# A planner that keeps GpSimd and VectorE apart in SBUF, block products that wait for their own sums, and new due times: a three-stage fp32 kernel on one Trainium2 core

## The chip, the core and the metric

The kernel runs on one core of a Trainium2 chip. The metric is the device time of one launch in microseconds (us). The time before is the median of 3 runs, 641.36 us (641.22, 641.36 and 764.43). One further execution was profiled; it took 639.59 us, and its span from the first to the last instruction is 637.8 us.

Engines are named as in the profile: PE is TensorE's matmuls, PEld its weight loads, DVE is VectorE, ACT is ScalarE, POOL is GpSimd, SP is the queue that issues DMAs.

## The reference

Three stages follow each other. Attention over 2 batches of 8 heads with 768 positions of 64 (a local band of 96 keys and 8 global keys, with a slope per head) gives x with 1536 rows of 512. Network 1 and network 2 each multiply by 512 x 2048, apply a function, and multiply by 2048 x 512.

```python
scores = scale * np.matmul(q, k.transpose(0, 1, 3, 2))
bias = -slopes[:, None, None] * dist[None, :, :]
scores = np.where(keep, scores + bias[None], -1000000000.0)
a = np.exp(scores - np.max(scores, axis=-1, keepdims=True))
x = np.matmul(a / (np.sum(a, axis=-1, keepdims=True) + 1e-09), v)   # heads joined: 1536 x 512
h = x @ moe_w_in
g = np.where(h >= 1, h, np.where(h <= -1, 0.0, (h + 1) ** 2 / 4))
x = g @ moe_w_out
h = x @ moe2_w_in
out = np.maximum(0.01 * h, h) @ moe2_w_out
```

The weights arrive as 64-bit numbers, q, k and v as 32-bit ones.

## The kernel before

**Numbers in two halves.** A 32-bit matmul operand is held as a rounded half `[:, 0]` and a rest `[:, 1]`; every product takes three matmuls (half by half, half by rest, rest by half). So each operand needs a copy (`copy`, L206 on ACT, L208 on DVE) and a subtraction (`sub`, L212 on DVE, L214 on POOL).

**Weights.** `job` turns one 128 x 512 piece of 64-bit weights into its halves. One DMA fills `raw`; `s0` (L407 or L409), `s01` (L413), `s1` (L417), `s11` (L421) build the number's upper part in `wd`, `s2` (L425) its lower part in `wr`, `s3` (L428, an integer addition that only POOL may do) adds them; `s4` and `s5` are the copy and the subtraction into the ring `w`. There are 64 such jobs. For network 2, `sums` (L468) also makes two combinations of each pair of pieces.

**Attention.** 24 calls of `quad` handle four heads of 128 positions each: transposes of k and q (L525), evictions into `ks` and `qt`, scores (L557), the table and the maximum (L566), exp (L575), row sums (L580, L581), normalization (L588 on DVE, L590 on POOL), transposes (L599), the product with v (L612), the eviction into `x`. Until the first four quads are through, the planner fills idle places of PE with dummy matmuls (L354).

**Network 1.** `step` does one 128-wide piece f of the hidden layer for one unit of rows: the hidden product (L693), `a1` (L700), the square (L708 or L710), `a2` (L715, which frees the PSUM bank), the two halves into `g`, then the output products (L755) into four banks; `finish` adds them to `part` (L792) and, at the last group, makes the halves of x anew. There are 6 units of 256 rows for the first 2 pieces f, then 3 units of 512 rows (twice, 7 pieces each). Unit 2 of 512 rows comes last.

**Passage and network 2.** For units 0 and 1 the hidden layer of network 2 is made from seven block products instead of eight. `x_sums` (L844) makes four sums t1, t2, t3, t4 of blocks of x and splits each into halves, t1 in the place of part of `x[1]`, t2, t3, t4 in the tiles `xt`. `two(j, True)` then runs, for each of 8 rounds j, seven products of six matmuls (L885) on four PSUM banks, with two VectorE additions from bank to bank between them (`cc`, L930, and `ce`, L933):

```python
p1 = add({PE: c6}, prod(Ba, wa, 0, x0, 0, True, False), d, w1 + xs, takes=[Ba, Bb, Bc, Be] + Hs)
p5 = add({PE: c6}, prod(Be, wc, 1, x1, 0, True, True), d + n7, [p1] + wx_op[j])
```

They go on in the order p2, p6 (t2), `cc`, p7 (t3), `ce`, p3, p4 (t4). `two(j, False)` does unit 2 with plain products (L952). Then come the activation (L896, L901) and the output products (L967); `finish` adds into `part` and, in the last round, writes out (L810, DMA).

**What sets the order.** Nothing above is issued as it stands. Each piece of work is an `Op` with a cost per engine that may do it, a due time (a table `DUE`, added to the due time of its step or round), the work that must precede it and the buffers that it takes and gives back. `Schedule.run` plays the program through with these costs: whenever an engine is idle, it gets the ready `Op` with the earliest due time whose buffers are free. The order so found is the order of each engine's queue on the chip; there only semaphores on data and buffers hold an instruction back, and the planned times play no part.

## Time and profile before

| | |
|---|---|
| median of 3 runs | 641.36 us |
| the profiled execution | 639.59 us, of which the span 637.8 us |
| busy PE / PEld | 615.7 us (97%) / 511.6 us (80%) |
| busy DVE / ACT / POOL | 500.7 us (79%) / 345.4 us (54%) / 291.0 us (46%) |
| mean granted TensorE clock | 0.984 of full speed |

Each share is a mean over the three stages, which differ. A dummy matmul counts as busy PE, and a matmul at the lower granted clock counts as busy for its longer time; so a view by stretch, with the granted clock beside the busy times, tells more than the page's first part. The mean of a group of instructions holds for the stretch that the view was asked for.

### The profile page before, as it was taken

The page shows a single profiled execution, that of the slowest core. Times are in us where ns is not written, and L with a number is a line of the kernel's source. Part 1 is how long each engine was busy: PE and PEld are TensorE (multiplying, and loading weights), DVE is VectorE, ACT ScalarE, POOL GpSimd, SP SyncE. Part 2 cuts the span into 40 slices and gives each one's busy share as a digit, 9 for nine tenths or more (in the row PEclk, how much of TensorE's full clock was granted, in tenths as well). Part 3 has the DMA queues.
Part 4 walks back from the last instruction along what each step waited for, and adds up shares of the span by engine and source line. Part 5 has one row for each costly group of instructions (what it writes and reads, how often), then busy time and mean ns, then how long its engine had stood idle before and what let it go on. Part 6 is the DMA issues. An engine that isn't in the chain of part 4 may idle for free.

```text
span 637.8 us, 9609 instructions
## 1 busy us (share of the span) xinstructions
PE 615.7 (97%) x3395; PEld 511.6 (80%) x3395; DVE 500.7 (79%) x985; ACT 345.4 (54%) x744; POOL 291.0 (46%) x314
## 2 busy tenths in 40 slices
PE   7999999999999999999999798999999999999995
PEld 5878887898688888888888686888888888888884
DVE  4899999979995649972559989668888888887653
ACT  3898898966464546553446445553536363534120
POOL 4477776447663234730116657306353536362000
PEclk7999999999999999999999988999999999999998
DMA  5974554113341203320012022102221212200014
GB/s 99 221 170 126 122 153 116 35 34 133 99 133 33 67 34 99 133 66 1 0 34 66 1 99 68 66 2 66 67 66 67 66 67 67 66 1 1 1 51 153
DMA packets 62346, 46.99 MB, mean 74 GB/s; under 512 B 40144, under 2 KB 56784, under 8 KB 62288
## 3 DMA queue, kind: packets, MB, share of 16 engines
q1 hardware_dynamic: 62288, 46.28, 25.0%
q8 instruction: 29, 0.48, 0.3%
q14 instruction: 29, 0.24, 0.1%
HBM read 43.12 MB, written 3.15 MB: 73 GB/s over the span
## 4 chain that ended last, share of the span: by engine, by line


## 5 line engine op out<-in xcount | busy, mean ns | idle before, releaser
L755 PE MATMUL bank<-g,w 128*128 128x512 f32 (+1 forms) x648 | 144.4, 369 | 0.0
L693 PE MATMUL bank<-x,w 128*128 128x512 f32 (+1 forms) x648 | 141.7, 368 | 2.2 <-POOL w L214 1.8
L693 PEld LDWEIGHTS bank<-x,w 128*128 128x128 f32 x648 | 111.8, 188 | 24.1 <-POOL w L214 2.9
L755 PEld LDWEIGHTS bank<-g,w 128*128 128x128 f32 x648 | 113.4, 189 | 21.3 <-issue 0.5
L428 POOL TENSOR_TENSOR wd<-wd,wr 128x512 int32<-128x512 int32 x64 | 88.9, 1395 | 77.2 <-DVE wd L421 72.5
L967 PE MATMUL bank<-w,g 128*128 128x512 f32 x312 | 81.8, 389 | 0.0
L792 DVE TENSOR_TENSOR part<-bank,part 128x512 f32<-128x512 f32 x96 | 65.1, 682 | 14.0 <-PE bank L755 8.9
L967 PE MATMUL bank<-w,w 128*128 128x512 f32 x264 | 70.6, 389 | 0.0
L700 ACT ACTIVATE t<-bank,half 128x512 f32<-128x512 f32 (+1 forms) x54 | 34.5, 639 | 63.5 <-PE bank L693 48.2
L214 POOL TENSOR_TENSOR g<-t,g 128x512 fp32r<-128x512 f32 (+1 forms) x32 | 37.9, 1185 | 67.9 <-ACT g L206 47.8
L967 PEld LDWEIGHTS bank<-w,g 128*128 128x128 f32 x312 | 58.6, 188 | 12.1
L206 ACT CAST w<-wd 128x512 fp32r<-128x512 f32 x50 | 31.0, 620 | 53.9 <-POOL wd L428 30.6
L206 ACT CAST g<-t 128x512 fp32r<-128x512 f32 (+1 forms) x73 | 43.0, 590 | 29.0 <-DVE t L901 13.4
L967 PEld LDWEIGHTS bank<-w,w 128*128 128x128 f32 x264 | 49.6, 188 | 10.3
L214 POOL TENSOR_TENSOR w<-wd,w 128x512 fp32r<-128x512 f32 x34 | 46.1, 1356 | 22.9 <-DVE w L208 12.9
L896 ACT ACTIVATE t<-bank 128x512 f32<-128x512 f32 x48 | 28.6, 597 | 51.4 <-DVE bank L933 25.9
L715 DVE SCALAR_TENSOR_TENSOR t<-bank,t 128x512 f32<-128x512 f32 (+1 forms) x54 | 33.7, 624 | 27.9 <-ACT t L708 25.9
L885 PE MATMUL bank<-x,w 128*128 128x512 f32 x192 | 52.1, 410 | 3.2 <-DVE t L715 3.2
L421 DVE SCALAR_TENSOR_TENSOR wd<-raw,wd 128x512 int32<-128x512 int32 x64 | 53.3, 845 | 0.5
L212 DVE TENSOR_TENSOR g<-t,g 128x512 fp32r<-128x512 f32 x48 | 42.8, 892 | 10.1 <-ACT g L206 9.3
L212 DVE TENSOR_TENSOR w<-wd,w 128x512 fp32r<-128x512 f32 x46 | 44.6, 978 | 6.5 <-ACT w L206 4.8
L425 ACT ACTIVATE wr<-raw 128x512 int32<-128x512 uint32 x64 | 43.1, 674 | 10.5 <-POOL wd L428 10.5
(113 smaller groups left out, 1012.8 us busy)
## 6 DMA issues: line engine op xcount, KB each, us to landing
raw<-in_moe_w_in_dram SPq DMA_DIRECT2D x32, 512.0 KB, 3.8
raw<-in_moe_w_out_dram SPq DMA_DIRECT2D x32, 512.0 KB, 3.5
kd<-in_k_dram SPq DMA_DIRECT2D x24, 128.0 KB, 3.2
qd<-in_q_dram SPq DMA_DIRECT2D x24, 128.0 KB, 3.2
vd<-in_v_dram SPq DMA_DIRECT2D x12, 256.0 KB, 3.8
out_dram<-part SPq DMA_DIRECT2D x11, 256.0 KB, 2.0
out_dram<-part SPq DMA_DIRECT2D x2, 128.0 KB, 3.1
vg<-in_v_dram SPq DMA_DIRECT2D x2, 64.0 KB, 3.6
```

The source lines that it names most:

```text
L206: A.copy(out=out_, in_=in_)
L212: V.tensor_tensor(out=out_, in0=a, in1=b, op=ALU.subtract)
L214: GP.tensor_tensor(out=out_, in0=a, in1=b, op=ALU.subtract)
L421: V.scalar_tensor_tensor(out=Dd.tile, in0=hl()[0], scalar=-0x40000000, in1=Dd.tile, op0=ALU.bitwise_and, op1=ALU.bitwise_or)
L425: A.activation(out=Rr.tile, in_=hl()[1], func=AF.Copy, scale=2.0 ** -29)
L428: GP.tensor_tensor(out=Dd.tile, in0=Dd.tile, in1=Rr.tile, op=ALU.add)
L693: T.matmul(out=Hb.tile[:, 0:n], lhsT=wi.tile[:, a, kk * P:(kk + 1) * P], rhs=x[r][:, b, kk, c0:c0 + n], start=(kk == 0 and a + b == 0), st ...
L700: A.activation(out=t, in_=h, func=AF.Relu, bias=half, scale=0.5)
L755: T.matmul(out=o[:, z * n:(z + 1) * n], lhsT=wo.tile[:, a, cc * P:(cc + 1) * P], rhs=Gt.tile[:, b, 0:n], start=st, stop=sp_)
L792: V.tensor_tensor(out=part[r][sl], in0=ac(), in1=part[r][sl], op=ALU.add)
L885: T.matmul(out=bank.tile, lhsT=w.tile[:, a, (2 * z + kk) * P:(2 * z + kk + 1) * P], rhs=xx()[:, b, kx + kk, :], start=st and kk == 0 and a ...
L967: T.matmul(out=Bo.tile, lhsT=Gt[z, r].tile[:, b, cb * P:(cb + 1) * P], rhs=wo[z].tile[:, a, :], start=(z == 0 and a + b == 0), stop=(z == ...
```

## The change

- `Schedule.run` gets a rule for SBUF: an `Op` of DVE that is not marked `ps` (has no operand in PSUM) starts only while POOL is idle in the plan, and an `Op` of POOL only when no such `Op` of DVE runs. 15 calls of `add` are marked.
- The planned costs of DVE and POOL are smaller (a 512-wide DVE operation from two SBUF tensors 0.60 us, was 0.64; a copy 0.33, was 0.43; POOL's 1.26, was 1.33).
- `s3` may go to DVE too.
- `x_sums` keeps a name for each sum, and each block product waits for its own: p1 for the first two blocks of unit 0 and for the first output products of unit 2's last group, p5 for t1, p2 for two blocks of unit 0, p6 for t2, p7 for t3, p3 for two blocks of unit 1, p4 for t4.
- Network 2's due times start earlier by `TWO`, and the whole table of due times is new.

```diff
@@ Schedule.run
+                        if e == DVE and not o.ps and busy[POOL] > now or e == POOL and held > now:
+                            kept.append(x)
...
+                            continue
...
+                    if e == DVE and not o.ps:
+                        held = end
@@ emit
     def dve(n, fast=False):
-        return 67 + (0.7 if fast else 1.12) * n
+        return 67 + (0.523 if fast else 1.044) * n
     def pool_tt(n):
-        return 200 + 2.2 * n
+        return 187 + 2.1 * n
...
+    z -= TWO
     for j in range(NJ):
@@ job
         def s3(e):
-            GP.tensor_tensor(out=Dd.tile, in0=Dd.tile, in1=Rr.tile, op=ALU.add)
+            (V if e == DVE else GP).tensor_tensor(out=Dd.tile, in0=Dd.tile, in1=Rr.tile, op=ALU.add)
...
-        e0 = add({POOL: pool_tt(DM)}, s3, due + DUE["s3"], [c1, r], gives=[Rr])
+        e0 = add(both(DM), s3, due + DUE["s3"], [c1, r], gives=[Rr])
@@ two
-            xs = [o for rr in (0, 256, 512, 768) for o in x2_op.get(rr, [])] + x2_op["sums"]
...
-            p1 = add({PE: c6}, prod(Ba, wa, 0, x0, 0, True, False), d, w1 + xs, takes=[Ba, Bb, Bc, Be] + Hs)
-            p5 = add({PE: c6}, prod(Be, wc, 1, x1, 0, True, True), d + n7, [p1] + wx_op[j])
+            p1 = add({PE: c6}, prod(Ba, wa, 0, x0, 0, True, False), d, w1 + [s_of[0, 0], s_of[0, 1]] + acc_op[0, last_g[0], LARGE[-1]],
+                     takes=[Ba, Bb, Bc, Be] + Hs)
+            p5 = add({PE: c6}, prod(Be, wc, 1, x1, 0, True, True), d + n7, [p1] + wx_op[j] + x2_op["t1"])
...
-            p7 = add({PE: c6}, prod(Bb, wc, 0, lambda: xt[1], 0, False, False), d + 4 * n7, [p6, cc])
+            p7 = add({PE: c6}, prod(Bb, wc, 0, lambda: xt[1], 0, False, False), d + 4 * n7, [cc] + x2_op["t3"])
...
-            p4 = add({PE: c6}, prod(Bb, wb, 1, lambda: xt[2], 0, False, True), d + 6 * n7, [p3, ce])
+            p4 = add({PE: c6}, prod(Bb, wb, 1, lambda: xt[2], 0, False, True), d + 6 * n7, [ce] + x2_op["t4"])
@@
-JTWO = 11218.0
-START = 9438.0
+JTWO = 9533.0
+TWO = 6956.0
+START = 4271.0
...
-DUE = {'b0': -23756.0, 'b1': 8444.0, 'b2': -94.0, 'b3': 5431.0, ...
+DUE = {'b0': -10861.0, 'b1': 24038.0, 'b2': 5854.0, 'b3': 8875.0, ...
```

By the number of instructions, POOL has 38 of the 64 integer additions `s3`, where it had all (DVE has the other 26), 26 of the 64 `s01`, where it had 38, and 58 of the 96 normalizations, where it had 66. In all it has 223 instructions instead of 315, DVE 1061 instead of 987, ACT 668 instead of 650. PE does the same matmuls, with 95 dummies instead of 83.

Three places show how instructions move. The first is PE's queue at the passage, from the hidden product whose bank p5 will use (unit 2, `x2`) to the second or third block product. Before:

```order
L693 MATMUL bank6_76<-x2_67,w0_7_2065 128x512 x12
L755 MATMUL bank7_77<-g1_95,w1_2_92 128x512 x3
L755 MATMUL bank4_74<-g3_97,w1_3_93 128x512 x3
L755 MATMUL bank1_71<-g1_95,w1_2_92 128x512 x3
L755 MATMUL bank2_72<-g3_97,w1_3_93 128x512 x3
L755 MATMUL bank4_74<-g2_96,w1_4_2066 128x512 x3
L755 MATMUL bank7_77<-g3_97,w1_3_93 128x512 x3
L885 MATMUL bank3_73<-x0_65,w0_1_87 128x512 x6
L755 MATMUL bank1_71<-g3_97,w1_3_93 128x512 x3
L755 MATMUL bank2_72<-g2_96,w1_4_2066 128x512 x3
L885 MATMUL bank6_76<-x1_66,w0_2_88 128x512 x6
```

And now (L707, L769 and L901 are the old L693, L755 and L885):

```order
L707 MATMUL bank5_75<-x2_67,w0_7_2094 128x512 x12
L769 MATMUL bank4_74<-g0_94,w1_3_93 128x512 x3
L769 MATMUL bank7_77<-g1_95,w1_4_2095 128x512 x3
L769 MATMUL bank6_76<-g1_95,w1_4_2095 128x512 x3
L769 MATMUL bank7_77<-g3_97,w1_5_2096 128x512 x3
L769 MATMUL bank0_70<-g1_95,w1_4_2095 128x512 x3
L901 MATMUL bank2_72<-x0_65,w0_0_86 128x512 x6
L769 MATMUL bank4_74<-g1_95,w1_4_2095 128x512 x3
L901 MATMUL bank5_75<-x1_66,w0_2_88 128x512 x6
L901 MATMUL bank2_72<-x0_65,w0_0_86 128x512 x6
```

Between that hidden product and p5, which takes its bank, stand 30 matmuls before and 24 now.

The second place is the same queue a little later, from p7 (`xt` 1) to p4 (`xt` 2) of the first round. Before:

```order
L885 MATMUL bank5_75<-xt1_2059,w0_2_88 128x512 x6
L755 MATMUL bank1_71<-g3_97,w1_7_2069 128x512 x3
L885 MATMUL bank0_70<-x1_66,w0_3_89 128x512 x6
L885 MATMUL bank5_75<-xt2_2060,w0_0_86 128x512 x6
```

Now:

```order
L901 MATMUL bank3_73<-xt1_2088,w0_2_88 128x512 x6
L769 MATMUL bank6_76<-g2_96,w1_6_2097 128x512 x3
L769 MATMUL bank0_70<-g3_97,w1_5_2096 128x512 x3
L901 MATMUL bank1_71<-x1_66,w0_3_89 128x512 x6
L769 MATMUL bank0_70<-g2_96,w1_6_2097 128x512 x3
L769 MATMUL bank4_74<-g3_97,w1_5_2096 128x512 x3
L769 MATMUL bank7_77<-g0_94,w1_7_2098 128x512 x3
L769 MATMUL bank4_74<-g2_96,w1_6_2097 128x512 x3
L769 MATMUL bank6_76<-g0_94,w1_7_2098 128x512 x3
L901 MATMUL bank3_73<-xt2_2089,w0_1_87 128x512 x6
```

Between p7 and p4 stand 9 matmuls before and 27 now.

The third place is PE's queue in a later round of network 2, again from p7 to p4. Before:

```order
L885 MATMUL bank1_71<-xt1_2059,w0_6_2064 128x512 x6
L967 MATMUL bank6_76<-w1_0_90,w1_4_2066 128x512 x3
L967 MATMUL bank6_76<-w1_1_91,g0_94 128x512 x3
L885 MATMUL bank3_73<-x1_66,w0_7_2065 128x512 x6
L967 MATMUL bank7_77<-w1_0_90,w1_4_2066 128x512 x3
L967 MATMUL bank7_77<-w1_1_91,g0_94 128x512 x3
L885 MATMUL bank1_71<-xt2_2060,w0_5_2063 128x512 x6
```

Now, from p6 (`xt` 0) on:

```order
L901 MATMUL bank2_72<-xt0_2087,w0_7_2094 128x512 x6
L983 MATMUL bank7_77<-w1_2_92,w1_3_93 128x512 x3
L983 MATMUL bank7_77<-w1_7_2098,w1_5_2096 128x512 x3
L901 MATMUL bank2_72<-xt1_2088,w0_6_2093 128x512 x6
L901 MATMUL bank1_71<-x1_66,w0_7_2094 128x512 x6
L901 MATMUL bank2_72<-xt2_2089,w0_5_2092 128x512 x6
```

Where 18 matmuls stood between p7 and p4, now 6 stand, in each of the seven rounds after the first. Between p6 and p7 stood 18 matmuls (30 in the first round); now there stand 6 in the first round and in three later ones, 12 in three and 24 in one.

## Rows read from the trace of the kernel before

**Rows 1.** The page, busy time of each engine, its share of the span, instructions.

```profile
PE 615.7 (97%) x3395; PEld 511.6 (80%) x3395; DVE 500.7 (79%) x985; ACT 345.4 (54%) x744; POOL 291.0 (46%) x314
```

**Rows 2.** Stretches of the span: length, busy time (instructions) per engine, granted clock.

```profile
core 0: us, PE busy (x) PEld busy (x) DVE busy (x) ACT busy (x) POOL busy (x), PEclk, DMA share, GB/s
9.30:43.20 33.90, 33.29 (x331) 27.32 (x331) 30.93 (x134) 28.69 (x104) 19.31 (x38) 0.90 0.84 191
43.20:139.00 95.80, 92.40 (x908) 80.74 (x907) 90.63 (x304) 84.38 (x256) 62.14 (x91) 1.00 0.40 104
139.00:355.00 216.00, 214.27 (x964) 177.07 (x963) 159.96 (x219) 112.24 (x185) 93.06 (x74) 1.00 0.21 66
...
365.00:371.00 6.00, 6.00 (x14) 4.73 (x15) 4.55 (x6) 1.31 (x3) 3.67 (x3) 0.50 0.29 87
...
384.00:392.00 8.00, 5.16 (x16) 3.77 (x15) 8.00 (x11) 4.31 (x8) 5.84 (x6) 0.79 0.21 67
392.00:631.20 239.20, 239.20 (x1056) 197.82 (x1054) 183.66 (x279) 102.38 (x173) 91.32 (x81) 1.00 0.16 54
```

**Rows 3.** What PE waited for: total us, times, longest.

```profile
PE bank L885 <- DVE t L715: 3.2, 1, 3.2
PE bank L885 <- DVE bank L933: 2.8, 1, 2.8
```

**Rows 4.** DVE's timeline before the first stall's end.

```profile
359.13 2.98 DVE L212 TENSOR_TENSOR xt<-part,xt 128x512 fp32r<-128x512 f32 x3
362.03 0.68 DVE L212 TENSOR_TENSOR g<-t,g 128x512 fp32r<-128x512 f32 x1
...
364.19 0.69 DVE L715 SCALAR_TENSOR_TENSOR t<-bank,t 128x512 f32<-128x512 f32 x1 [0.21 <-ACT t L708]
```

**Rows 5.** ACT's timeline at the same place.

```profile
362.81 0.69 ACT L700 ACTIVATE t<-bank,half 128x512 f32<-128x512 f32 x1 [6.12 <-DVE g L212]
```

**Rows 6.** DVE's timeline before the second stall's end.

```profile
384.72 1.52 DVE L409 TENSOR_SCALAR wd<-raw 128x512 int32<-128x512 int32 x1
386.16 0.41 DVE L417 TENSOR_SCALAR wd<-wd 128x512 int32<-128x512 int32 x1
386.50 0.69 DVE L933 TENSOR_TENSOR bank<-bank,s 128x512 f32<-128x512 f32 x1
```

**Rows 7.** Operations on the tiles x, w, wd, part: duration ns min/median/max.

```profile
L212 DVE TENSOR_TENSOR w<-wd,w x46: 677/693/1783, 139.6 to 586.3; 128x512 fp32r<-128x512 f32 x46
L421 DVE SCALAR_TENSOR_TENSOR wd<-raw,wd x64: 661/686/1787, 35.2 to 573.7; 128x512 int32<-128x512 int32 x64
L428 POOL TENSOR_TENSOR wd<-wd,wr x64: 1270/1295/1747, 39.5 to 574.6; 128x512 int32<-128x512 int32 x64
L792 DVE TENSOR_TENSOR part<-bank,part x96: 673/681/692, 192.6 to 614.9; 128x512 f32<-128x512 f32 x96
```

**Rows 8.** A later round: DVE's `ce` and PE's p7 and the blocks behind it.

```profile
412.09 1.52 PE L885 MATMUL bank<-xt,w 128*128 128x512 f32 x6
413.45 1.52 PE L967 MATMUL bank<-w,w 128*128 128x512 f32 x6
...
413.65 0.70 DVE L933 TENSOR_TENSOR bank<-bank,s 128x512 f32<-128x512 f32 x1 [4.74 <-PE bank L885]
```

**Rows 9.** Groups of DVE instructions in the attention stage, 9.3 to 139 us: busy us, mean ns.

```profile
L588 DVE TENSOR_SCALAR sm<-sm,st 128x256 f32<-128x256 f32 x24 | 10.7, 484 | 0.0
L580 DVE TENSOR_SCALAR st<-st 128x4 f32<-128x4 f32 x24 | 8.1, 338 | 0.0
L208 DVE COPY part<-bank 128x512 f32<-128x512 f32 x3 | 2.0, 679 | 0.0
L208 DVE CAST ks<-bank 128x256 fp32r<-128x256 f32 x4 | 1.6, 412 | 0.0
```

**Rows 10.** DVE's row sums (L580), same stretch: duration ns min/median/max.

```profile
L580 DVE TENSOR_SCALAR st<-st x24: 150/164/1270, 19.4 to 129.9; 128x4 f32<-128x4 f32 x24
```

**Rows 11.** DVE's timeline, the shortest pair of normalizations.

```profile
44.12 0.63 DVE L588 TENSOR_SCALAR sm<-sm,st 128x256 f32<-128x256 f32 x2
```

More of the change, by code (lines that the diff above doesn't have):

```diff
@@ L52 @@
 class Op:
-    __slots__ = ("costs", "fn", "prio", "takes", "gives", "waits", "users", "at", "done", "tail")
+    __slots__ = ("costs", "fn", "prio", "takes", "gives", "waits", "users", "at", "done", "tail", "ps")
 class Schedule:
@@ L68, in __init__, with add @@
         self.fill = None
-    def add(self, costs, fn, prio, after=(), takes=(), gives=(), tail=0.0):
+    def add(self, costs, fn, prio, after=(), takes=(), gives=(), tail=0.0, ps=False):
         o = Op()
-        o.costs, o.fn, o.prio, o.gives, o.tail = costs, fn, prio, gives, tail
+        o.costs, o.fn, o.prio, o.gives, o.tail, o.ps = costs, fn, prio, gives, tail, ps
         o.takes = [(a, sum(b.ring is a.ring for b in takes[:y])) for y, a in enumerate(takes)]
@@ L435, in job @@
         a = add({SP: 1460}, load, due + DUE["wl"], [prev], takes=[R], tail=DLAT)
-        b = add({ACT: act(DM, False), DVE: dve(DM, True)}, s0, due + DUE["s0"], [a], takes=[Dd])
+        b = add({ACT: act(DM, False), DVE: dve(DM, True)}, s0, due + DUE["s0"], [a] + line("s0"), takes=[Dd])
+        chain["s0"] = b
         b = add({POOL: pool_ts(DM), DVE: dve(DM, True)}, s01, due + DUE["s01"], [b])
@@ L440, in job @@
         r = add({ACT: act(DM, False)}, s2, due + DUE["s2"], [a], takes=[Rr])
-        e0 = add({POOL: pool_tt(DM)}, s3, due + DUE["s3"], [c1, r], gives=[Rr])
-        e1 = add({ACT: act(DM, False), DVE: dve(DM, True)}, s4, due + DUE["s4"], [e0], takes=[W])
+        e0 = add(both(DM), s3, due + DUE["s3"], [c1, r], gives=[Rr])
+        e1 = add({ACT: act(DM, False), DVE: dve(DM, True)}, s4, due + DUE["s4"], [e0] + line(("w", o)), takes=[W])
+        chain["w", o] = e1
         e2 = add(both(DM), s5, due + DUE["s5"], [e1], gives=[] if m and not o else [Dd])
@@ L625, in quad @@
         o1 = add({PE: 4 * 109}, tr, d + DUE["tr"], [o0, o_id, before], takes=[b1, h1, Qt], gives=[Kd, Qd])
-        oh = add({ACT: 2 * act(n), DVE: 2 * dve(n)}, ev_hi, d + DUE["hi"], [o1])
-        ol = add({DVE: 2 * dve(n)}, ev_lo, d + DUE["lo"], [oh], gives=[b1, h1])
+        oh = add({ACT: 2 * act(n), DVE: 2 * dve(n)}, ev_hi, d + DUE["hi"], [o1], ps=True)
+        ol = add({DVE: 2 * dve(n)}, ev_lo, d + DUE["lo"], [oh], gives=[b1, h1], ps=True)
         f = 4 * G
@@ L648, in quad @@
         add({NONE: 0}, lambda e: None, d - 2900, o9, gives=[Sm, St])
-        oa = [add({ACT: act(2 * nb * P), DVE: dve(2 * nb * P)}, p_ev(y), d + DUE["pev"] + y, [o9[y]], gives=[b3[y], h3[y]])
+        oa = [add({ACT: act(2 * nb * P), DVE: dve(2 * nb * P)}, p_ev(y), d + DUE["pev"] + y, [o9[y]], gives=[b3[y], h3[y]], ps=True)
               for y in range(2)]
@@ L660, in quad @@
         vx_op[i] = ob
-        oc = add({ACT: act(n), DVE: dve(n)}, lambda e: copy(e, hi, two(b4.tile[:, 0:n])), d + DUE["xhi"], [ob])
+        oc = add({ACT: act(n), DVE: dve(n)}, lambda e: copy(e, hi, two(b4.tile[:, 0:n])), d + DUE["xhi"], [ob], ps=True)
         x_op[i] = add({DVE: dve(n)}, lambda e: sub(e, lo, two(b4.tile[:, 0:n]), hi.bitcast(F32)), d + DUE["xlo"], [oc],
-                      gives=[b4, h4])
+                      gives=[b4, h4], ps=True)
     last_g = [len(GROUPS) - 1, NJ - 1]
@@ L767, in step @@
         out_op[m, g, u] = now_
+        if first:
+            acc_op[m, g, u] = now_
         chain["o"] = now_[-1]
@@ L796, in finish @@
             before = list(x2_op.get(("r", r), [])) if m else [o_late if r == 2 else None]
-            o = add({ACT: act(512), DVE: dve(512)}, f0, d + 600 + cb, [after] + before, gives=[B_])
+            o = add({ACT: act(512), DVE: dve(512)}, f0, d + 600 + cb, [after] + before, gives=[B_], ps=True)
             for kk in keys:
@@ L857, in parts @@
                 x2_op.setdefault(("r", rr), []).append(o2)
[L858 removed]
+            x2_op.setdefault(name, []).append(o2)
         t1 = add(both(512), c_((0, kk), (1, kk), (0, kk)), d + 4000, [b_op[1, kk], s_of[0, kk]])
@@ L908, in act_ @@
             o = add({ACT: act(512)}, a1, dd + DUE["b1"], after, takes=[Tt])
-            o = add({DVE: dve(512)}, a2, dd + DUE["b2"], [o], gives=gives)
+            o = add({DVE: dve(512)}, a2, dd + DUE["b2"], [o], gives=gives, ps=True)
             o3 = add({ACT: act(512, False), DVE: dve(512, True)}, a3, dd + DUE["b3"], [o], takes=[G_])
@@ L930, in two @@
+            s5 = add({ACT: act(512), DVE: dve(512)}, lambda e: copy(e, S5.tile, Be.tile), d + n7 + 1400 + DUE["b0"], [p5], takes=[S5], ps=True)
+            p2 = add({PE: c6}, prod(Ba, wa, 1, x0, 2, False, True), d + 2 * n7, [p1, cp, s_of[0, 2], s_of[0, 3]])
+            p6 = add({PE: c6}, prod(Bb, wd_, 0, lambda: xt[0], 0, False, False), d + 3 * n7, [cp] + wx_op[j] + x2_op["t2"])
             cc = add({DVE: dve(512)}, lambda e: V.tensor_tensor(out=Bc.tile, in0=Bb.tile, in1=S5.tile, op=ALU.add),
-                     d + 3 * n7 + 1400 + DUE["b0"], [p6, s5])
```

51 lines of the change are left out of this document (26 added, 25 removed).

## The prediction

> **What bounds the kernel now.** I read the page's first part first: PE is busy for 615.7 of 637.8 us [rows 1]. No other engine can be the bound over the whole, so a change of order can win only what PE loses. The table by stretches shows where that is [rows 2]. From 392 to 631.2 us (network 2) PE is never idle and has the full clock: nothing is to be had there, only to be lost. From 139 to 355 us 1.7 us are idle. In the attention stage, 43.2 to 139 us, PE is idle for 3.4 us, but DVE is busy for 90.6 of 95.8 and ACT for 84.4: that stage runs at the pace of these two. Up to 43.2 us PE is kept busy with dummies. The clearest loss lies between 361 and 392 us, at the passage between the networks: the list of PE's waits has two single stalls there, 3.2 and 2.8 us [rows 3], and behind each the granted clock falls, to 0.50 of full speed for 365 to 371 us, to 0.79 in 384 to 392 us [rows 2].
>
> What ends these stalls is read from DVE's own timeline. The first belongs to p5, which needs the PSUM bank of the last hidden product; `a2` (L715) frees it at 364.19 + 0.69 = 364.88 us [rows 4]. `a2` is late because ACT's `a1` starts at 362.81, after DVE's subtraction `g` at 362.03 + 0.68 [rows 4, 5], which stood behind three subtractions of `xt` that took 2.98 us. The second belongs to p4, which waits for `ce` (L933): DVE gets to it at 386.50, after one conversion of 1.52 us [rows 6].
>
> Why is 1.52 us long? DVE's 512-wide subtractions from SBUF take 677 ns at least and 693 in the median, but up to 1783; the addition that has one operand in PSUM (L792) stays within 673 to 692 in all 96 cases. POOL's addition goes from 1270 to 1747 [rows 7]. The long ones are a short one plus about the length of a POOL operation: DVE and POOL wait for each other when both want SBUF, and PSUM operands are exempt. That is what the planner now models. The Trainium skill, "SBUF — State Buffer", section "Who interferes with whom", says the same (the later of the two blocks until the first has finished, and issue order decides which one that is); the 677 and 1783 ns agree. By this rule nothing in a queue's order holds the two apart, since no semaphore joins them; that is rival 1 below, which I price from rows.
>
> **Passage: what is regained.** Idle 3.2 + 2.8 = 6.0 us [rows 3]. The lower clock: 6 us at 0.50 lose 3.0, 8 us at 0.79 lose 1.7, together 4.7 [rows 2]; both drops stand behind a long stall, so I let them go with the stalls. Whole price: 10.7 us.
>
> What is late next? A block of six matmuls, p7 or the three and three behind it, takes 413.45 - 412.09 = 1.36 us [rows 8], so one matmul 0.227. Between the hidden product and p5 stand 24 matmuls now, 5.4 us, instead of 30, 6.8 us. In them ACT must do `a1` (0.69 as in row 362.81) and the square, DVE `a2` (0.69), after DVE has freed the tile `t`. In DVE's new queue some 20 operations of 0.4 to 0.7 us lie between the last additions of unit 1 and this `a2`, about 15 us, all of x's and `xt`'s subtractions among them; counted from those additions on, I get `a2` done about 1.5 us before PE asks for it if nothing is blocked. One blocked operation costs up to 1783 - 677 = 1.1 us, so two use that up. Lower bound of a rest: 0; upper: the stall stays at 3.2 us with its 3.0 of clock. I take back 1.5. Between p7 and p4 stand 27 matmuls (6.1 us) instead of 9 (2.0), against the 2.1 us that DVE was late there: this stall should be gone. The naming of sums lets p1 and p5 go before t2 to t4 are ready; in the new queue four plain output blocks lie between anyway, so this costs nothing and its gain is in those numbers. **Passage: -9.2 us.**
>
> **Attention stage.** Its end is set by DVE (and ACT), so I count DVE's work up to the last eviction into x, in both orders, by row durations. Added: 8 casts of `ks` and `qt` at 0.41 = 3.3 [rows 9]; 4 copies of `part` at 0.68 = 2.7; 4 copies of `pT`, same form and so 0.68, less two half ones, 1.9; 10 normalizations at 0.48 less 2 small ones, 4.1; the table of biases and two weight subtractions, about 3.5. Gone: 4 + 2 + 3 conversions, casts and copies, the rest of the small ones, together about 8. Sum +7 us of DVE's own work. Gone from POOL: some 23 of its 128 instructions, about 15 of the 81.5 us that it is busy between 9.3 and 139 us [rows 2], a fifth. DVE's waits for POOL in this stage: 24 normalizations have a mean of 484 ns [rows 9], where two in a row take 0.63 us at the shortest, 0.32 each [rows 11]; the 24 row sums have 338 [rows 9], with a minimum of 150 [rows 10]. That is 24 x 0.16 + 24 x 0.19 = 8 us, and I take as much again for all other forms: 17 us. If the waits only shrink with POOL's share they fall to 14, and the stage's end comes 7 - 3 = 4 us later. If the plan keeps the two apart on the chip as well, they fall to some 4, and it comes 13 - 7 = 6 us earlier. By that end PE has done 15 more output matmuls (9 of 0.227, 6 of half that), 2.7 us of work ahead. So between +1.3 and -8.7; the middle is **-3.5 us**. ACT has 7 instructions more there, about 2 us, which it can hold in its 11 idle us. The first hidden product now stands behind eight quads instead of six and 12 more dummies are planned: in a stage that DVE ends, this moves PE's idle time forward and adds none.
>
> **Network 1 after the attention.** Idle 1.7 us before; POOL's 26 fewer integer additions go to DVE. No trace shows that form on DVE: its nearest rows are the 0.686 of an integer operation with two SBUF operands and POOL's own 1.295 [rows 7]; I take 0.75, nearer to the same engine. 25 of them over 490 us are 19 us for an engine with 160 busy of 216 and 184 of 239 us: hidden. **0 us**, bounds +-2.
>
> **Network 2.** The seven products are a chain through DVE. After p7 `ce` starts at 413.65, just as p7's time ends (412.09 + 1.52), and takes 0.70 [rows 8]: ready at 414.35, while PE comes to the place behind one block of six at 414.81. Where one such block stands between p7 and p4 (seven rounds now, 18 matmuls before) the margin is 0.4 us. Rounds with only PSUM additions between `cc` and `ce` hold it; where weight and `g` subtractions stand there one blocked operation (1.1 us) breaks it. Lower bound 0, upper 11 places (seven of `ce`, four of `cc` with one block) x (1.1 - 0.4) = 8. I take two rounds: **+1.5 us**. The rest of the chain (banks, the tail with its last addition and DMA) stays.
>
> **Sum.** -9.2 - 3.5 + 0 + 1.5 = -11.2 us. The profiled execution took 639.6, so it would take 628.4; the median of the three runs, 641.4, lies 1.8 above it: **630 us**.
>
> **Rivals.** *1, the plan's separation does not survive on the chip.* POOL starts whenever its semaphores let it, earlier than planned, and blocks DVE as before. For it: no instruction is added that would hold POOL. Against: POOL has a third fewer instructions. Then the first stall stays with half its clock (passage -10.7 + 4.7 = -6), the attention stage gives +1.3, network 2 +3: 641.4 - 1.7 = 640; 636 to 645. *2, it survives whole.* Passage -10.7, attention -8.7, network 2 +0.5: -18.9, 622.5; 619 to 626. For it: POOL's planned 1.26 for a 512-wide addition is near the undisturbed 1.27 to 1.295 [rows 7], so the plan and the chip agree on when POOL ends; against it, an `Op` early by a few tenths of a us shifts all that follows. *3, slower: network 2's chain breaks.* It decides from the point where DVE reaches `ce` more than 0.4 us after p7's end. If it comes 2.1 us late in each of the seven rounds, as it did before the second stall, PE loses 7 x 1.7 = 12 us, and if each is followed by a lower clock as behind that stall, 7 x 1.7 = 12 more: 641.4 - 12.7 + 24 = 653; 648 to 658. Against it: in all later rounds before the change PE never waited, and PSUM operands are not blocked.
>
> **How the numbers follow.** Forecast 0.53 (own range 626 to 635), rival 1 0.21, rival 2 0.20, rival 3 0.06. Two per cent, about what a measurement of this kernel can tell from no change, is 12.8 us: below 628.5 lie rival 2 and 0.15 of the forecast, 0.35; above 654.2 lies 0.03 of rival 3, and I add 0.02 for bounds that I have not seen: 0.05; within, 0.60. The range 620 to 645 leaves out rival 3 and the edges of the others.
>
> **What would show it.** Right: no wait of PE above 1.5 us between the networks, a granted clock of 1.00 there; DVE's conversions and subtractions with a mean near 0.45 and 0.70 and fewer above 1 us; DVE's busy time below 500.7 us though it has 74 more instructions; PE idle in network 2 by less than 2 us. Wrong: a stall of p5 on `a2` as before; the last attention product of PE (near 138 us) later than before; a wait of L901 on `ce` in each round; or PE waiting in network 1 for weights, which the new split between DVE and POOL could make late and which I have put at nothing.

## The result, and the profile after

| | before | after |
|---|---|---|
| median | 641.29 us of 4 runs | 624.58 us of 4 runs (624.25 to 625.27) |
| ratio | | 0.9746, 95% interval 0.9727 to 0.9765 |
| profiled execution, its span | 639.59, 637.8 us | 625.27, 623.5 us |
| mean granted clock | 0.984 | 0.991 |

The change is faster by 2.5%, and the time lies 5.4 us below the forecast of 630, in its range of 620 to 645. One of the runs of before (764.43 us) lies far above the other three and is not in the ratio.

The page's first part, of after, answers to [rows 1]:

```profile
PE 610.4 (98%) x3407; PEld 508.6 (82%) x3407; DVE 483.5 (78%) x1059; ACT 353.0 (57%) x762; POOL 187.8 (30%) x222
```

DVE has 74 records more and is busy for 17.2 us less. PE, with 12 more dummies, is busy for 5.3 us less: the low clock at the passage is gone. The stretches of after, columns as in [rows 2]:

```profile
43.20:139.00 95.80, 94.16 (x935) 82.73 (x934) 87.94 (x315) 84.92 (x259) 49.53 (x72) 1.00 0.41 104
139.00:355.00 216.00, 215.78 (x973) 179.22 (x974) 158.61 (x262) 117.18 (x195) 44.81 (x37) 1.00 0.21 66
355.00:392.00 37.00, 37.00 (x163) 30.32 (x162) 33.61 (x53) 23.43 (x41) 17.49 (x16) 1.00 0.23 72
392.00:617.10 225.10, 224.69 (x990) 185.36 (x989) 171.50 (x288) 97.03 (x165) 59.70 (x52) 1.00 0.17 57
```

Between 355 and 392 us PE is busy for 37.00 of 37.00 us at the full clock. What PE still waits for, all of its list but the two waits of the first 13 us (first transfer, and a constant), columns as in [rows 3]:

```profile
PE bank L613 <- DVE sm L602: 2.1, 3, 0.8
PE bank L901 <- DVE bank L946: 0.4, 1, 0.4
PE bank L707 <- DVE w L222: 0.2, 1, 0.2
```

Both waits of [rows 3] are gone. The lines of after have other numbers than before: L901 was L885, L707 was L693, L613 the transposes L599, and of the releasers L946 was `cc` (L930), L222 the subtraction L212, L602 the normalization L588. DVE's and POOL's operations on SBUF, against [rows 7] (duration min/median/max):

```profile
L222 DVE TENSOR_TENSOR w<-wd,w x54: 659/686/1792, 71.4 to 583.9; 128x512 fp32r<-128x512 f32 x54
L432 DVE SCALAR_TENSOR_TENSOR wd<-raw,wd x64: 659/683/1785, 42.8 to 567.7; 128x512 int32<-128x512 int32 x64
L439 POOL TENSOR_TENSOR wd<-wd,wr x38: 1266/1296/1886, 45.2 to 568.4; 128x512 int32<-128x512 int32 x38
L439 DVE CUSTOM_DVE_ANT_0 wd<-wd,wr x26: 677/684/1098, 134.8 to 542.1; 128x1024 uint16<-128x1024 uint16 x26
L808 DVE TENSOR_TENSOR part<-bank,part x96: 673/691/692, 185.1 to 600.8; 128x512 f32<-128x512 f32 x96
```

The longest are as long as before, so DVE and POOL still meet; only how often has changed. To count it in any trace I take DVE's operations that read SBUF alone, call one blocked when it lasts over 100 ns longer than the lower quartile of its operation and shape, and add up what it lasts longer. Before, 141 of 462 are blocked and lose 86 us in all; after, 55 of 516 and 30 us.

That POOL is what blocks them can be read off the same two traces. In 140 of the 141 before, and in all 55 after, a POOL operation was running when DVE's began, and it ended before DVE's did; what DVE's lost is the rest of that POOL operation less 0.13 to 0.22 us (in nine of ten). Of all DVE operations on SBUF alone, 180 in the kernel before and 68 in after began with at least 0.1 us of a POOL operation still to go, and all blocked ones are among them. Of the operations with an operand in PSUM 177 began so in the kernel before, and none of them is blocked. That fewer begin so isn't only because POOL does less: 180 of 462 are 39%, with POOL busy for 46% of the span, 68 of 516 are 13%, with POOL busy for 30%, and operations with an operand in PSUM begin so as often as before (191 of 445).

**Where the time went.** The last matmul ends at 617.08 us instead of 631.21, 14.1 us earlier. The passage gives 10.7 of it: 6.0 us of stalls and 4.7 of clock [rows 2, 3], all gone. The attention stage gives 1.6: its last matmul ends 1.1 us later (138.90 against 137.77), but by then PE has done 9 matmuls of 0.227 and 6 of half that more, 2.7 us. Network 2 takes back 0.4, the one wait of L901 above. The remaining 2.2 us are network 1's, of which 1.5 are seen as idle time of PE (1.7 before, 0.2 now); counted from each matmul's start to the next one's, over the median for its shape, PE loses 2.4 us less there. The tail is 0.2 us shorter.

### The profile page after: what moved, and what is told of

Its sections match the earlier page's. It is cut to its first block, busy times and chain, and to the rows that moved or that the text cites. A ratio compares the mean times of both kernels' runs of the same rounds, so it can differ in the third digit from the quotient of the medians.

```text
span 623.5 us, 9587 instructions
## 1 busy us (share of the span) xinstructions
PE 610.4 (98%) x3407; PEld 508.6 (82%) x3407; DVE 483.5 (78%) x1059; ACT 353.0 (57%) x762; POOL 187.8 (30%) x222
## 4 chain that ended last, share of the span: by engine, by line
## 5 line engine op out<-in xcount | busy, mean ns | idle before, releaser
L769 PE MATMUL bank<-g,w 128*128 128x512 f32 (+1 forms) x648 | 143.5, 368 | 0.0
L707 PE MATMUL bank<-x,w 128*128 128x512 f32 (+1 forms) x648 | 140.1, 367 | 0.2 <-DVE w L222 0.2
L769 PEld LDWEIGHTS bank<-g,w 128*128 128x128 f32 x648 | 112.6, 188 | 20.5 <-issue 0.5
L707 PEld LDWEIGHTS bank<-x,w 128*128 128x128 f32 x648 | 112.0, 188 | 20.8 <-DVE w L222 0.7
L439 POOL TENSOR_TENSOR wd<-wd,wr 128x512 int32<-128x512 int32 x38 | 53.3, 1407 | 153.9 <-DVE wd L432 144.1
L216 ACT CAST w<-wd 128x512 fp32r<-128x512 f32 x60 | 37.1, 620 | 45.9 <-PE bank L983 17.6
L222 DVE TENSOR_TENSOR g<-t,g 128x512 fp32r<-128x512 f32 (+1 forms) x57 | 39.4, 695 | 16.2 <-ACT g L216 15.9
L432 DVE SCALAR_TENSOR_TENSOR wd<-raw,wd 128x512 int32<-128x512 int32 x64 | 49.7, 784 | 0.3
L901 PE MATMUL bank<-x,w 128*128 128x512 f32 x192 | 48.4, 389 | 0.0
L589 ACT ACTIVATE sm<-sm,st 128x256 f32<-128x256 f32 (+1 forms) x96 | 46.1, 490 | 1.8 <-DVE st L580 1.7
L224 POOL TENSOR_TENSOR w<-wd,w 128x512 fp32r<-128x512 f32 x26 | 33.9, 1306 | 43.9 <-ACT w L216 26.5
L968 PE MATMUL bank<-x,w 128*128 128x512 f32 x192 | 45.3, 389 | 0.0
L418 ACT ACTIVATE wd<-raw 128x512 f32<-128x512 f32 x58 | 38.6, 672 | 10.0 <-DVE w L222 7.3
```

The lines of the kernel that those rows point to most:

```text
L216: A.copy(out=out_, in_=in_)
L222: V.tensor_tensor(out=out_, in0=a, in1=b, op=ALU.subtract)
L432: V.scalar_tensor_tensor(out=Dd.tile, in0=hl()[0], scalar=-0x40000000, in1=Dd.tile, op0=ALU.bitwise_and, op1=ALU.bitwise_or)
L439: (V if e == DVE else GP).tensor_tensor(out=Dd.tile, in0=Dd.tile, in1=Rr.tile, op=ALU.add)
L589: A.activation(out=Sm.tile[:, a, 0:W], in_=Sm.tile[:, a, 0:W], func=AF.Exp, scale=-1.0, bias=St.tile[:, 0, a:a + 1], accum_out=St.tile[:, ...
L707: T.matmul(out=Hb.tile[:, 0:n], lhsT=wi.tile[:, a, kk * P:(kk + 1) * P], rhs=x[r][:, b, kk, c0:c0 + n], start=(kk == 0 and a + b == 0), st ...
```

## The experiments

Three theories stood against each other. **Lock**: DVE's operations that are held up by POOL made PE wait, and the rule for SBUF is what took that away. **Order**: the new due times and waits moved what PE needs far enough ahead, as the passage term of the prediction argued with its distances (24 matmuls, 27 instead of 9). **Fit**: rule and due times work only together. The count of blocked operations is that defined above.

| kernel | us | ratio to before, interval | blocked, us lost |
|---|---|---|---|
| before | 640.6 to 641.4 | | 141, 86 |
| after | 624.58 | 0.9746 [0.9727, 0.9765] | 55, 30 |
| after, no rule | 680.45 | 1.0611 [1.0573, 1.0648] | 168, 103 |
| before, new dues | 659.11 | 1.0285 [1.0256, 1.0313] | 168, 105 |
| before, GpSimd short | 621.63 | 0.9705 [0.9676, 0.9734] | 27, 14 |
| after, GpSimd short | 621.28 | 0.9690 [0.9663, 0.9716] | 10, 4 |
| before, rule and costs | 625.88 | 0.9776 [0.9748, 0.9803] | 61, 33 |
| after, old dues | 623.38 | 0.9723 [0.9696, 0.9751] | 47, 20 |
| after, old wait of p1 | 624.39 | 0.9740 [0.9718, 0.9763] | 54, 30 |
| after, s3 on POOL | 624.22 | 0.9745 [0.9722, 0.9769] | 59, 32 |
| before, costs alone | 655.00 | 1.0223 [1.0201, 1.0245] | 147, 86 |
| before, rule, old costs | 626.15 | 0.9780 [0.9758, 0.9803] | 51, 25 |
| before, half of the rule | 629.65 | 0.9836 [0.9812, 0.9859] | 128, 78 |
| after, no rule, GpSimd short | 630.63 | 0.9838 [0.9810, 0.9867] | 37, 21 |

### The order kept, POOL taken out of the way

The planner doesn't see how much an instruction really works on. So these two kernels keep every queue's order and change POOL's operations alone:

```diff
-            GP.tensor_tensor(out=out_, in0=a, in1=b, op=ALU.subtract)
+            n = out_.shape[-1] if new else 32
+            GP.tensor_tensor(out=out_[..., 0:n], in0=a[..., 0:n], in1=b[..., 0:n], op=ALU.subtract)
...
-            GP.tensor_tensor(out=Dd.tile, in0=Dd.tile, in1=Rr.tile, op=ALU.add)
+            GP.tensor_tensor(out=Dd.tile[:, 0:32], in0=Dd.tile[:, 0:32], in1=Rr.tile[:, 0:32], op=ALU.add)
```

> The kernel before with each engine's order as it was, but most of GpSimd's large operations work on 32 columns (integer additions, clamps, normalizations, and subtractions except for the first into each place), so its results are not the reference's and GpSimd occupies SBUF for a small part of its former time. Theory Lock: DVE's long operations are nearly all gone, p5 no longer waits for a2 by more than 1 us and p4 for ce by less than 1.3, both low clocks go, PE's 4.7 us of waits for POOL's weight halves go too: 628 to 632. Rival Order: what makes a2 and ce late is what stands ahead of them in DVE's queue, also at their undisturbed length: the stalls stay above 1.5 us each and the time is 636 to 640.

Measured 621.63 us, 3% below before and even below the range that Lock gave. The page's first part:

```profile
PE 608.4 (98%) x3395; PEld 508.4 (82%) x3395; DVE 437.3 (71%) x985; ACT 342.5 (55%) x744; POOL 136.1 (22%) x314
```

DVE runs the same 985 instructions on the same shapes in 437.3 us instead of 500.7 [rows 1]: 63 us of its time before were waits for POOL. (The 4.7 us of waits for POOL's weight halves in the expectation count PE and PEld together; PE's own list has 1.8.) At the place of the first stall DVE's timeline is now

```profile
349.86 1.94 DVE L217 TENSOR_TENSOR xt<-part,xt 128x512 fp32r<-128x512 f32 x3
351.72 0.68 DVE L217 TENSOR_TENSOR g<-t,g 128x512 fp32r<-128x512 f32 x1
...
353.88 0.69 DVE L722 SCALAR_TENSOR_TENSOR t<-bank,t 128x512 f32<-128x512 f32 x1 [0.21 <-ACT t L715]
...
369.24 0.70 DVE L940 TENSOR_TENSOR bank<-bank,s 128x512 f32<-128x512 f32 x1 [0.25 <-PE bank L892]
```

and PE's, with p5, p7 and p4:

```profile
354.63 1.65 PE L892 MATMUL bank<-x,w 128*128 128x512 f32 x6 [0.57 <-DVE t L722]
...
367.68 1.52 PE L892 MATMUL bank<-xt,w 128*128 128x512 f32 x6
369.04 0.84 PE L762 MATMUL bank<-g,w 128*128 128x512 f32 x3
369.72 1.52 PE L892 MATMUL bank<-x,w 128*128 128x512 f32 x6
371.08 1.52 PE L892 MATMUL bank<-xt,w 128*128 128x512 f32 x6
```

These are the lines of [rows 4, 5] in the same order. The three subtractions of `xt` take 1.94 us instead of 2.98 and p5 waits 0.57 us instead of 3.2. `ce`, which DVE reached at 386.50, 4.2 us behind p7's end at 380.83 + 1.52 = 382.35, now starts 0.04 us behind it (369.24 against 367.68 + 1.52), and p4 follows without a wait with the same 9 matmuls in between. So the old order was good at both places, and Order falls for the passage. What this kernel can't tell apart is DVE's waits from POOL's results that come sooner, since short operations on POOL bring both. For the passage the trace of before does: DVE had no idle time from 354.29 to 363.98 us, ahead of the first stall, and between 330 us and the second stall it waited for POOL's results twice, 1.4 us before 367.95 (behind the first stall) and 0.6 us before 379.00, 7 us ahead of the `ce` that came 4.2 us late. Elsewhere PE itself waited for POOL's results, in network 1 and in the attention stage:

```profile
PE bank L693 <- POOL w L214: 1.8, 3, 1.0
PE bank L599 <- POOL sm L590: 1.3, 3, 0.7
```

How much of these 3.1 us is due to POOL being held up by DVE was not tried.

> The changed kernel with its order as it is, but most of GpSimd's large operations work on 32 columns (integer additions, clamps, normalizations, and subtractions except for the first into each place), so its results are not the reference's. It tells what the DVE operations that still wait for POOL cost the changed kernel. Theory Lock: in the attention stage DVE sets the pace and its remaining waits of about 6 us are worth 2 to 4 us there: 620 to 623. Rival Order: PE has no more to win, since it idles for 2.7 us in all after the first transfer: within 1 us of the changed kernel, 623.5 to 625.5.

Measured 621.28 us: Lock's figure, 3.3 us below after. DVE's busy time:

```profile
PE 608.8 (98%) x3407; PEld 508.6 (82%) x3407; DVE 461.6 (74%) x1059; ACT 350.4 (57%) x762; POOL 92.4 (15%) x222
```

With the same order DVE is busy for 21.9 us less than in after (483.5), where it was 63.4 for before. With POOL out of the way the two orders take the same time, 621.6 and 621.3. What the change gains can so be read as a part of these 19 us, and the rest, 3.3 us, as what the new order still leaves.

### The rule taken out

```diff
-                        if e == DVE and not o.ps and busy[POOL] > now or e == POOL and held > now:
-                            kept.append(x)
-                            if len(kept) > 40:
-                                break
-                            continue
```

> The changed kernel with the planner's rule for SBUF switched off; dues, waits, costs and the new place of s3 stay. Theory Lock (the gain comes from fewer DVE operations that wait for a POOL operation): the plan lets the two overlap again, DVE's SBUF operations above 1 us come back towards the number of the kernel before, a stall of PE above 1.5 us returns at the passage or PE idles some 2 us after the attention, and the time is 631 to 638. Rival Order (the new dues and waits put a2 and ce far enough ahead of PE's need, whatever DVE's operations last): PE's waits between the networks stay under 1 us each and the time is 624 to 628.

Measured 680.45 us, far outside both. Blocked operations come back (168, 103 us against 86), but the kernel is 56 us behind after, where before is 16 behind. PE's waits:

```profile
PE bank L978 <- DVE part L803: 11.8, 5, 2.7
PE bank L896 <- DVE t L724: 9.0, 1, 9.0
```

Four of the waits of L978 are of 2.7 us each, at 506, 541, 577 and 613 us, once in a round. DVE's timeline ahead of the first, and what PE then does:

```profile
504.08 0.96 DVE L213 CAST w<-wd 128x512 fp32r<-128x512 f32 x1
504.96 1.77 DVE L217 TENSOR_TENSOR g<-t,g 128x512 fp32r<-128x512 f32 x1
506.65 1.48 DVE L476 TENSOR_TENSOR wd<-wd 128x256 f32<-128x256 f32 x1
508.06 0.68 DVE L803 TENSOR_TENSOR part<-bank,part 128x512 f32<-128x512 f32 x1
```

```profile
508.79 1.43 PE L978 MATMUL bank<-w,w 128*128 128x512 f32 x5 [2.72 <-DVE part L803]
```

From the start of the first of the three operations ahead of L803 to that of L803 it takes 4.0 us, where their undisturbed lengths (0.42, 0.69 and 0.42 in after's rows of the same forms) make 1.5: 2.5 of the 2.7 us. This is the same picture as at the stalls of before, in each round.

To part the blocked operations from the order itself, POOL was made short in this kernel too, as above.

> The changed kernel without the rule (680 us) with its order as it is, but most of GpSimd's large operations work on 32 columns (integer additions, clamps, normalizations, and subtractions except for the first into each place), so its results are not the reference's. Theory Lock (the order is good but for DVE operations that POOL holds up): 621 to 627, the stall of 9 us at the passage and those of 2.7 us on part in network 2 are gone. Rival Order (the new dues without the rule give an order that is late by itself): the stalls stay at more than half their length and the time is above 640.

Measured 630.63 us, between the two. The stalls on `part` are gone; the wait at p5 is

```profile
PE bank L904 <- DVE t L732: 2.6, 1, 2.6
```

instead of 9.0. So of the 59 us between the kernel without the rule and the changed kernel with POOL short (621.28), 50 go with POOL, and 9.3 (630.63 against 621.28) are the order's own. Both theories missed their ranges, and both hold a part, Lock the larger by far. The kernel without the rule keeps the smaller costs, which lose time by themselves (costs alone, below); they were not taken back together with the rule.

### The due times alone, the costs alone

The kernel before with the new table and TWO, nothing else:

```diff
+    z -= TWO
...
-JTWO = 11218.0
-START = 9438.0
+JTWO = 9533.0
+TWO = 6956.0
+START = 4271.0
...
-DUE = {'b0': -23756.0, 'b1': 8444.0, 'b2': -94.0, 'b3': 5431.0, ...
+DUE = {'b0': -10861.0, 'b1': 24038.0, 'b2': 5854.0, 'b3': 8875.0, ...
```

> The kernel before with the new table of due times, START, STEP, JTWO, TWO and the like, and nothing else of the change (no rule, old costs, s3 on POOL alone, each product waits for all sums). Theory Lock: the times at which things were due were not what stalled PE, and the stalls between the networks stay: 636 to 645. Rival Order: the stalls at p5 and p4 are gone and most of the gain is there: 625 to 631.

Measured 659.11 us, slower than either theory allowed: 168 blocked operations, PE waits 6.3 us for `a2` and 7.5 us in five waits on additions to `part`. Order falls again: the new due times by themselves lose 18.5 us.

The kernel before with the new costs, nothing else:

```diff
-        return 67 + (0.7 if fast else 1.12) * n
+        return 67 + (0.523 if fast else 1.044) * n
...
-        return 200 + 2.2 * n
+        return 187 + 2.1 * n
...
-        return 240 + 0.87 * n
+        return 230 + 0.834 * n
```

> The kernel before with the smaller planned costs of DVE and POOL alone; no rule, old dues, old waits, s3 on POOL. Theory Rule (the rule itself is the cause; costs that suit undisturbed operations make the plan worse where operations still block each other): about 140 blocked DVE operations, stalls of PE as before or worse, 640 to 660. Rival Costs (part of the gain is that the plan knows the real durations): 626 to 637.

Measured 655.00 us, as theory Rule said, with 147 blocked operations and the stalls of [rows 3] grown:

```profile
PE bank L885 <- DVE bank L933: 5.6, 1, 5.6
PE bank L885 <- DVE t L715: 4.2, 1, 4.2
```

Here a plan that believes in undisturbed operations without keeping them undisturbed is worse than one with padded costs.

### The rule alone

Everything of the change taken back but the rule, the marks and the costs (the old dues, the old waits and their chain of products, s3 on POOL, and without the lines that keep the copies into `w` and the `s0` in their order; these lines are part of the change too, though its description above doesn't list them). Against the kernel before, besides the costs above and the 15 marks `ps=True`:

```diff
+                        if e == DVE and not o.ps and busy[POOL] > now or e == POOL and held > now:
+                            kept.append(x)
...
+                            continue
...
+                    if e == DVE and not o.ps:
+                        held = end
```

> The kernel before with the planner's rule for SBUF and the smaller planned costs that go with it; the old dues, the old waits, s3 on POOL alone. Theory Lock alone (the rule is the cause, and any table of dues will do): the blocked DVE operations fall from 141 to under 80 and the time is 625 to 633. Rival Fit (the dues have to be found with the rule in force; a table that was found without it makes a poor order under it, as the new table without the rule made 680 us): blocked operations fall just the same, but PE waits for additions to part, for a2 or for weights, and the time is 640 to 665.

Measured 625.88 us, Lock's range: 15.5 us of the gain of 16 to 17 are here. PE's waits, again all but those of the first 13 us, two of 0.3 and 0.6 us on `pT` and one of 0.3 us on weights:

```profile
PE bank L704 <- DVE w L222: 1.1, 1, 1.1
PE bank L610 <- DVE sm L599: 1.0, 2, 0.9
...
PE bank L898 <- DVE bank L944: 0.5, 1, 0.5
```

With the old costs, 5 to 30% longer, under the rule:

> The kernel before with the rule for SBUF and the marks, and the old, longer planned costs; old dues, old waits, s3 on POOL. Theory Rule: 624 to 629, since a plan that holds DVE and POOL too long leaves room between them; blocked operations under 75. Rival Costs: with costs that are 5 to 30% too long the planned gaps drift away from those on the chip, more than 90 blocked operations and 630 to 640.

Measured 626.15 us with 51 blocked operations: the same. The costs matter only where the rule is missing; Costs falls.

With half of the rule, so that POOL may start in the plan while DVE runs:

```diff
-                        if e == DVE and not o.ps and busy[POOL] > now or e == POOL and held > now:
+                        if e == DVE and not o.ps and busy[POOL] > now:
```

> The kernel before with the rule and the smaller costs, but only its first half: DVE's SBUF operations wait in the plan for POOL to be idle, POOL may start while one of them runs. Theory One side (what costs is a DVE operation behind a POOL operation of 1.3 us; a POOL operation behind a DVE operation of 0.4 to 0.7 us costs nothing, POOL having time): 625 to 630 and under 90 blocked operations. Rival Both sides (POOL then starts later on the chip than in the plan, ends later, and DVE runs into its end): 631 to 640 and over 100 blocked operations.

Measured 629.65 us with 128 blocked operations: the time is One side's, the count Both sides'. Three quarters of the gain come with hardly fewer blocked operations. So the count alone doesn't decide the time; where the blocked operations fall does. Of the 78 us lost, 39 are in network 1 after the attention (40 before) and 27 in network 2 from 392 us on (19 before), where DVE has time; up to 139 us it is 6 instead of 15, at the passage, 355 to 392 us, 6 instead of 11, and PE has no wait above 0.1 us there. The plan also gives POOL more of the work:

```profile
PE 612.2 (98%) x3411; PEld 510.7 (81%) x3411; DVE 481.6 (77%) x942; ACT 343.4 (55%) x736; POOL 349.2 (56%) x365
```

PE then waits once for POOL's half of `g`, 1.8 us at 352.5 us, and behind it the granted clock is 0.57 for 4 us:

```profile
355.00:359.00 4.00, 4.00 (x12) 3.14 (x11) 3.23 (x4) 2.52 (x5) 3.39 (x3) 0.57 0.00 0
```

That wait and 1.7 us of clock are about the 3.8 us by which half of the rule is slower than the whole. Why fewer waits fall in the places that matter was not tried further.

### The other parts, each taken back

The new table and TWO are taken back (the diff of the new due times above, reversed, with TWO = 0):

> The changed kernel with the old table of due times (START, STEP, JTWO and the like of before, TWO = 0). Theory Lock alone: 625 to 633, few blocked operations. Rival Fit: few blocked operations too, but waits of PE on DVE's additions to part or on a2, and 640 to 665.

Measured 623.38 us: Lock; the rule works with a table that was found without it. The interval overlaps that of after, so the new due times bring nothing under the rule, and Fit falls in the direction that mattered: the rule needs no new table. Only the reverse holds, the new table does harm without the rule.

The wait of p1 alone is taken back:

> The changed kernel with p1 of each round waiting for all sums and all halves of x of units 0 and 1, as before; the other products keep what they wait for. Theory of the prediction (this part costs and gains nothing by itself, since four plain output blocks lie between t1 and the others): 624 to 627, no PE wait above 0.5 us at the passage. Rival Waits (p1 now has to come after t4, and the plan has no work left to put there): a stall of 1 to 4 us at the first p1 with a lower clock behind it, 627 to 633.

```diff
-            p1 = add({PE: c6}, prod(Ba, wa, 0, x0, 0, True, False), d, w1 + [s_of[0, 0], s_of[0, 1]] + acc_op[0, last_g[0], LARGE[-1]],
+            p1 = add({PE: c6}, prod(Ba, wa, 0, x0, 0, True, False), d, w1 + xs + acc_op[0, last_g[0], LARGE[-1]],
```

(`xs` is the list of all halves and sums, as in the kernel before.)

Measured 624.39 us, no wait of PE at the passage; the naming of sums costs and gains nothing here, as predicted.

The integer addition goes back to POOL:

```diff
-        e0 = add(both(DM), s3, due + DUE["s3"], [c1, r], gives=[Rr])
+        e0 = add({POOL: pool_tt(DM)}, s3, due + DUE["s3"], [c1, r], gives=[Rr])
```

> The changed kernel with s3 on POOL alone, as before, everything else as it is: 26 additions of 1.3 us go back to POOL. Theory Place (26 operations fewer on POOL are part of what keeps DVE free; under the rule POOL then has to wait for gaps of DVE and the weights come late): PE waits for weights in network 1 and 627 to 636. Rival: the rule finds the room, POOL is busy for 30% only, and the time is 624 to 626.

Measured 624.22 us: the rival. POOL is busy for 205.2 us instead of 187.8, 59 operations are blocked instead of 55, and PE waits in network 1 for 0.2 us in all.

## Why the prediction came out as it did

The time lies in the stated range, but below the 626 to 635 that the forecast gave itself and inside the 619 to 626 of rival 2, which had 0.20. A time within two per cent of before had been given 0.60, a lower one 0.35; it came out lower. The terms up to the last matmul make 2.9 of the 5.4 us and the tail 0.2. The other 2.4 come from the profiled executions, which the terms are read from: that of before lies 1.7 us below its median, that of after 0.7 above.

| term | predicted | measured |
|---|---|---|
| passage | -9.2 | -10.7 |
| attention | -3.5 (+1.3 to -8.7) | -1.6 |
| network 1 | 0 (+-2) | -2.2 |
| network 2 | +1.5 (0 to 8) | +0.4 |
| sum, to the last matmul | -11.2 | -14.1 |

**Passage: the size held, half of its reason did not.** I let the whole price, stalls and clock, go and took 1.5 back for one or two blocked operations; nothing was left to take back. The step "between p7 and p4 stand 27 matmuls instead of 9 ... this stall should be gone" named a cause that isn't one: with the old 9 matmuls and undisturbed DVE operations there is no stall either (GpSimd short), and the old dues and waits under the rule leave a single one of 0.5 us there (rule and costs). The rows that carried the right reason were [rows 4, 6]: the 2.98 us of three subtractions that take 1.94 undisturbed, and the 1.52 us of a conversion that takes 0.42.

**Attention: the bound was made on the wrong engine.** -8.7 was counted in DVE's time. But PE was idle there for 3.4 us, and PE sets the end: even with POOL short and the order of before, the last attention matmul comes 4.7 us earlier (133.09 against 137.77), and PE is then busy for 95.8 of 96 us (row below). DVE's gain beyond that is slack. In after that matmul comes 1.1 us later than before, which the prediction had named as a sign of being wrong; the sign left out the 2.7 us of other work that PE has done by then, which its own term counted. The waits did shrink as taken, the row sums' mean from 338 to 188 ns and the normalizations' from 484 to 402 [rows 9]:

```profile
L602 DVE TENSOR_SCALAR sm<-sm,st 128x256 f32<-128x256 f32 x34 | 11.9, 402 | 0.0
L594 DVE TENSOR_SCALAR st<-st 128x4 f32<-128x4 f32 x24 | 4.5, 188 | 0.0
```

The kernel before with GpSimd short, columns as in [rows 2]:

```profile
43.00:139.00 96.00, 95.78 (x941) 85.16 (x940) 86.09 (x314) 86.17 (x261) 39.99 (x94) 1.00 0.40 104
```

The 12 dummies, put at nothing, are 1.9 us of PE's work here (16.2 against 14.3); whether they cost any was not tried.

**Network 1: the idle time was read and not counted.** 1.7 us stood in the text as idle and no gain was taken from it; 1.5 went. The gain of 2.2 lies just outside the bounds of +-2. The integer addition on DVE takes 0.684 us, just under the lower of the two rows that I bounded it by (0.686), where I took 0.75, and it is hidden, as said; so is POOL's (s3 on POOL).

**Network 2.** Two of the 11 close places were to fail; one did, by 0.4 us, and as argued: one blocked operation, the second row here, stood a little ahead of a `cc` (L946), and p7 waited for it. POOL's integer addition had begun at 442.34 us.

```profile
442.34 1.68 POOL L439 TENSOR_TENSOR wd<-wd,wr 128x512 int32<-128x512 int32 x1 [3.15 <-DVE wd L432]
442.78 1.79 DVE L222 TENSOR_TENSOR w<-t,w 128x512 fp32r<-128x512 f32 x1
446.03 0.68 DVE L946 TENSOR_TENSOR bank<-bank,s 128x512 f32<-128x512 f32 x1
446.76 1.66 PE L901 MATMUL bank<-xt,w 128*128 128x512 f32 x6 [0.39 <-DVE bank L946]
```

At `ce` the margin of 0.4 us held in all seven later rounds: it starts within 0.06 us of p7's end and is ready 0.44 to 0.48 us before PE begins p4, also in the three rounds where weight subtractions stand between `cc` and `ce`. In one of these an operation there was blocked (a clamp of 1.15 us instead of 0.42) and cost nothing.

**The rivals.** Rival 1, that the separation doesn't survive on the chip, is wrong by the count (141 to 55) and by the time. Rival 2, that it survives whole, is not right either, though 624.6 lies in its 619 to 626: a third of DVE's waits for POOL is left (21.9 of 63.4 us by the pairs with GpSimd short), and whole it would be worth 621.3. Rival 3's chain never broke. How much there was to win could have been read off PE: its idle time after 43 us, 3.4 + 1.7 + 6.0, and 4.7 of clock make 15.8 us [rows 2, 3]; cutting POOL's operations gives 18.0 (spans of 637.8 and 619.8 us). Idle time counts a wait too low, since the records of matmuls overlap (one lasts 0.389 us, the next starts after 0.227). Counted from start to start, as above, PE loses 0.5 us less up to 43 us, 4.3 less in the attention stage, 2.1 in network 1 and 11.1 at the passage, which is the 18.0.

The rule of the Trainium skill that the prediction weighed ("SBUF — State Buffer", "Who interferes with whom") is borne out by the pairs: with the order untouched, DVE's time falls by 63 us when POOL's operations are cut, and the additions to `part` with a PSUM operand stay between 673 and 693 ns in all runs. What spoke against the change by it, that nothing in a queue's order holds the two apart, is true of the 55 operations that are still blocked; the order, with less work on POOL, did bring their number down from 141.

**What stays open.** Why these 55 are blocked (the plan's times drift from the chip's, or a releasing semaphore comes late) was not tried; a version that holds POOL by a semaphore was not built. The change's new due times and its own waits are free in time but not shown to be needed. Old dues with the rest of the change gave 623.38 us, the lowest of the kernels that leave nothing out, and not distinguishable from after.

## What to carry to other kernels

Where GpSimd and VectorE share a kernel, compare minimum and maximum of each VectorE form that reads and writes SBUF: a maximum of about the minimum plus one GpSimd operation was the sign here that a plan which treats the two as independent is wrong. Making them exclusive in the plan was worth 15.5 us, the new table of priorities under it nothing. Cut the suspected engine's operations to a few columns with the order kept: this one run gave the whole price (3%) and showed that the order was not to blame. In a kernel that one engine bounds, judge the gain of a stage by that engine's idle time and lost clock there, not by the time that its neighbours get back; here this came out at 15.8 us, a little under the 18.0 that were to be had.
